# Lightning attention and a low-rank mixer on one core: new start of the pipeline and a new order of the attention steps

## The chip, the core and the metric

The kernel runs on one NeuronCore of a Trainium2 chip. The core has five engines that run side by side, each with an instruction queue of its own: TensorE (PE: matmuls, transposes as matmuls, and the weight loads that belong to them, shown apart as PEld), VectorE (DVE), ScalarE (ACT), GpSimd (POOL) and SyncE (SP), which here issues DMA transfers. ScalarE also issues some. An instruction waits in its queue until the semaphores it names have been raised, and what stands behind it on that engine waits with it.

The metric is the time of one execution on the device in microseconds (us). For the kernel before, three executions and one with the profiler are at hand. A trace of the profiled one gives the start and duration of each instruction, and for idle time of an engine a guess at what ended it.

## The reference

Two blocks follow each other. The first is a linear attention with a decay per head (4 batches, 8 heads, 768 positions, 64 channels), computed blockwise; the second mixes positions with a low-rank pair U, V and then applies a two-layer network.

```python
# attention, per block of positions (the kernel uses blocks of 128)
intra = einsum('bhic,bhjc->bhij', qb, kb) * Dmask        # Dmask[i, j] = lam ** (i - j), i >= j
intra = einsum('bhij,bhjd->bhid', intra, vb)
inter = einsum('bhid,bhde->bhie', qb * lam_pow, kv_state)
out   = intra + inter
kv_state = lam_block * kv_state + einsum('bhsd,bhse->bhde', kb * rev_pow, vb)
# bridge: x[b, s, h*64 + d]; then the mixer
u = x + (x.transpose(0, 2, 1) @ U @ V).transpose(0, 2, 1)
return u + maximum(u @ w_ch1, 0) @ w_ch2
```

q, k, v and lam are fp32. U (768x32), V (32x768), w_ch1 and w_ch2 are float64; the kernel loads them as pairs of 32-bit words and rebuilds fp32 values from exponent and mantissa bits.

## The kernel before

**Stages.** The attention front handles 24 steps s = 0..23 (4 batches of NT = 6 tiles of 128 positions); c = s % 6 is the place in the batch. After it come the first product (u @ w_ch1, in units of 12 or 24 matmuls of 128x512) and the second (with w_ch2). The trace puts the front at 0 to about 111 us, the first product's units from there. The change touches the front alone.

**What one step does.** The lists that the loop over s builds (`pieces`, printed below) are written out by hand, and each engine runs its instructions in that order. For step s, and always one step ahead for some of the work:

- `prep(s+1)`: PE transposes q and k of the next tile into one PSUM tile (`pqk`, L419); ScalarE copies them out as `qt`, `kt` (L425); SP issues the load of a later q.
- `scale(s+1)`: GpSimd makes `qs` = qt times powers (L450) and `ks` of the tile after (L439).
- `intra(s)` (L524): PE multiplies the masked scores `sm` with v into `px`. `inter(s)` (L536): PE adds qs times the state `kv` to `px`. `state(s)` (L489): PE makes k'v into `pkv`, VectorE forms the next state (L495, L497 or L500). In which order these three stand depends on s: `inter_first` lists the steps in which `inter` goes first, steps up to 6 put `state` ahead of `intra`, later ones `intra` ahead of `state`.
- `next_v`: ScalarE issues the next load of v. `take_x` (L546): ScalarE copies px out as x. `fade` (L459): ScalarE scales the state.
- `scores(s+1)` (L466): PE makes the scores `pss` of the next tile. `masked(s+1)` (L475): VectorE multiplies them with the mask, in two halves of 0.65 us, into `sm`.
- `low`, `low_rows`, `next_of_low` (L556, L589, L597, L598, L608): once per batch, the product with U, its rounding and its spreading. `mix`, `mixed` (L631, L643): the product with V, added to x. `turn`, `split`, `turned` (L694, L708, L709, L701): transposes of u for the first product.

**Conversions.** `weight_steps` turns float64 words into fp32 in steps: load(s) from SP (L149), `one` on VectorE (L170, L158) with two exponent operations on ScalarE (L177, L178), `two` (L188), `three` (L196, which waits for L178), `four` (L201). For V more follow: `five` (L787), the high part (ScalarE, L794), and the low part in two row groups, `low(1)` on VectorE and `low(3)` on GpSimd (both L798). A table gives each step a number, and `aside(s)` runs the steps of that number: before `masked(s+1)` in some steps, behind it in others. `late` is the place at which the ScalarE part runs; for U and V that is one step later or at the end of the same one.

**The start.** lam (8 numbers) is loaded into one partition, a matmul with a row of ones (L855) copies it to all 128, and VectorE moves it to `lamb` (L857). From that come the mask (eight scans, L367) and the powers (L379). Meanwhile PE runs matmuls of zeros, `keep_busy` (L402): two of 128x128, then after L855 two of 128x128 and nine of 16x16. The first loads are issued in the order q0 (two halves), q1, v0, k2, v1, q2, U, k3 on SP; lam, k0 (two halves), k1 on ScalarE's queue. Buffers: three for q, three for v, four for k.

Of the kernel before, what the change touches and what calls it, by code (L numbers as in the profile page):

```python
# [8 lines left out]
FP32 = mybir.dt.float32  # L9
# [5 lines left out]
P = 128  # L15
# [3 lines left out]
def kernel(  # L19
# [28 lines left out]
    nc = tc.nc  # L48

    B, H, S, D = q.shape  # L50
    HP = H // 2
    NT = S // P
# [7 lines left out]
    NS = B * NT  # L60
# [28 lines left out]
    def on_scalar(what):  # L89
        if late and late[0] is None:  # L90
            late.append(what)
        else:
            what()


    def set_ends(t):
        nc.vector.memset(t[:, 0:1], 1151.0)
        nc.vector.memset(t[:, 1:2], 255.0 * (1 << 23))
        ends.append(t)
# [202 lines left out]
    consts = att_ctx.enter_context(tc.tile_pool(name="consts", bufs=1))  # L302
# [7 lines left out]
    def two_banks(name, tag):  # L310
        return psf.tile([P, 2, N], FP32, tag=tag, name=name)
# [7 lines left out]
    def bank(shape, name, tag):  # L319
        return psa[0].tile(shape, FP32, tag=tag, bufs=2, name=name)  # L320

    lamb = consts.tile([P, H], FP32, name="lamb")
# [74 lines left out]
    def keep_busy(n):  # L397

        out = two_banks("idle", "pm")[:, 0]
        for i in range(n):  # L400
            k = P if i < 2 else D // 4
            nc.tensor.matmul(  # L402
                out=out[0:k, 0:k], lhsT=blank[:, 0:k], rhs=blank[:, 0:k], start=True, stop=True
            )
# [101 lines left out]
        del raw[s, "v"]  # L506
        load_next("v", nc.scalar)

    inter_first = (NT - 1, NT + 1, NS - 1)

    def px_of(s):
        if "px" not in st[s]:
# [38 lines left out]
    def low(b):  # L551

        pp = two_banks("pp", "px")[:, 0, 0:P] if b < B - 1 else bank([P, P], "pp", "b2")
        for c in range(NT):
            for g in range(G):
                nc.tensor.matmul(  # L556
                    out=pp[g * R : (g + 1) * R, :], lhsT=u_w[:, c, :],
                    rhs=xs[b * NT + c][:, g * P : (g + 1) * P],
                    start=(c == 0), stop=(c == NT - 1),
                )  # L560
        pps[b] = pp
# [152 lines left out]

    splits = {}

    pieces = [("prep", 0), ("next_k", 0), ("third_v", 0), ("scale", 0), ("scores", 0), ("masked", 0)]
    for s in range(NS):
        b, c = divmod(s, NT)
        done = s - NT - 1  # L720
        more = s + 1 < NS
        turns = done > 0 and (done - 1) // TG < FG
        mixes = 0 <= done < NS - NT - 1
        rows = c == 0 and b > 0
        step = [("fade", s)] * (c > 0)
        step += [("mix", done)] * (mixes and c != 1) + [("turn", done - 1)] * turns
        step += [("next_of_low", b - 1)] * rows
        step += [("split", done - 1)] * turns
        step += [("prep", s + 1)] * more
        step += [("mix", done + 1)] * (not more)  # L730
        step += [("scale", s + 1)] * more
        step += [("mixed", done)] * (mixes and c != 1)
        step += [("late", s - 1)] * (1 < s < NT - 1 or s > NT)
        step += [("turned", done - 2)] * (done > 1 and c == 1)
        step += [("mixed", done + 1)] * (not more)
        both = [("intra", s), ("state", s)] + [("v_low", s)] * (s == NT)
        if s in inter_first:
            step += [("inter", s)] + both + [("next_v", s)]
        else:
            step += (both if s > NT else both[1:] + both[:1]) + [("next_v", s), ("inter", s)]  # L740
        step += [("take_x", s)]
        step += [("next_of_low", b - 1)] * rows
        step += [("late", s)] * (s < 2 or s in (NT - 1, NT))
        step += [("turned", done - 1)] * (done > 0 and c > 0)
        step += [("mix", done), ("mixed", done)] * (mixes and c == 1)
        step += [("scores", s + 1)] * more
        step += [("low", b)] * (more and c == NT - 1)
        step += [("aside", s)] * (0 < s < NT - 2 or s > NT)
        step += [("masked", s + 1)] * more
        step += [("low_rows", b)] * (more and c == NT - 1)  # L750
        step += [("aside", s)] * (s in (0, NT - 2, NT - 1, NT))
        step += [("store", done)] * (done >= 0 and done // TG < FG)
        step += [("next_k", s)] * (s > 0)
        pieces += step
    waiting = {name: list(range(NS)) for name in "qkv"}

    def load_next(name, engine=nc.sync):
        if waiting[name]:
            load(name, waiting[name].pop(0), engine)


    run = {
        "prep": prep, "fade": fade, "scores": scores, "masked": masked, "inter": inter, "take_x": take_x,
        "intra": intra, "state": state,
        "low": low, "low_rows": low_rows, "next_of_low": next_of_low, "mix": mix, "turn": turn,
        "mixed": mixed, "store": store, "next_v": next_v, "split": lambda s: splits.pop(s)(),
        
        "next_k": lambda s: load_next("k"), "third_v": lambda s: load_next("v", nc.scalar), "scale": scale, "turned": lambda s: turned.pop(s)(),
    }
    def v_steps():  # L770

        st = {}

        def dst():
            if "v" not in st:
                st["v"] = wconv.tile([P, C], FP32, tag="wf", name="vf")[0 : 2 * R, 0:SH]
            return st["v"]

        def parts(gs):
            for half in range(2):  # L780
                rows, cols = slice(half * R, (half + 1) * R), slice(half * SH, (half + 1) * SH)
                for g in gs:
                    yield v_hl[g * R : (g + 1) * R, cols], rows

        def five():
            st["t"] = t = wconv.tile([P, C], FP32, tag="wt", name="vt")[0 : 2 * R, 0:SH]
            nc.vector.tensor_scalar(  # L787
                t.bitcast(U32), st["v"].bitcast(U32), HI, None, ALU.bitwise_and
            )
            on_scalar(high)  # L790

        def high():
            for out, rows in parts((0, 2)):
                nc.scalar.copy(out, st["t"][rows])  # L794

        def low(g, engine):
            for out, rows in parts((g,)):
                engine.tensor_tensor(  # L798
                    out=out, in0=st["v"][rows], in1=st["t"][rows], op=ALU.subtract
                )  # L800

        halves = [moe_V[:, half * SH : (half + 1) * SH] for half in range(2)]
        return weight_steps(dst, halves, SH, 2 * R, in_parts=True) + [
            five, lambda: v_low.append(lambda: low(1, nc.vector)), lambda: low(3, nc.gpsimd),
        ]

    v_low = []
    run["v_low"] = lambda s: v_low.pop()()


    u_side = weight_steps(
        lambda: u_w.rearrange("p c r -> p (c r)"), moe_U.rearrange("(c p) r -> p c r", p=P), NT * R
    )
    side = {}
    for steps, at in (
        (u_side, (-1, 1, 1, 2, 2)),
        (v_steps(), (0, 0, 3, 3, 4, 4, 4, 5, 5)),
        (w1_steps(0, True, True), (8, 9, 10, 11, 12, 14, 15, 16, 17, 17, 20, 21)),
        (w1_steps(1, True, True), (14, 15, 16, 17, 18, 22, 23, NS, NS, NS, NS, NS)),
    ):  # L820
        assert len(steps) == len(at)
        for step, n in zip(steps, at):
            side.setdefault(n, []).append(step)

    def aside(s):
        late.insert(0, None)
        for step in side.pop(s, ()):
            step()
        late.pop(0)
# [5 lines left out]

    ordered = ctx.enter_context(ExitStack())
    ordered.enter_context(tc.manual_schedule())
    lam_row = consts.tile([1, H + P], FP32, name="lam_row")
    blank = x_pool.tile([P, C], FP32, tag="x", name="blank")[:, 0:P]
    nc.vector.memset(blank, 0.0)  # L840
    nc.vector.memset(lam_row[:, H:], 1.0)
    set_ends(vp[:, S + C : S + C + 2].bitcast(FP32))
    nc.scalar.dma_start(out=lam_row[:, 0:H], in_=lam.unsqueeze(0))
    load_next("q", nc.sync)
    load_next("k", nc.scalar)
    load_next("q")
    load_next("k", nc.scalar)
    for name in "vkvq":
        load_next(name)
    aside(-1)  # L850
    load_next("k")
    make_identity(nc, ident)
    pl = two_banks("pl", "pss")[:, 0, 0:H]
    keep_busy(2)
    nc.tensor.matmul(out=pl, lhsT=lam_row[:, H:], rhs=lam_row[:, 0:H], start=True, stop=True)  # L855
    keep_busy(3 + 8)
    nc.vector.tensor_copy(out=lamb, in_=pl)  # L857
    constants()
    powers()
    nc.vector.tensor_copy(out=rev, in_=mask[:, :, :, P - 1])  # L860
# [646 lines left out]
```

## Time and profile before

| | |
|---|---|
| three executions | 635.54, 637.08, 637.39 us (median 637.08) |
| the profiled execution | 635.38 us, of which its span (first to last instruction) 633.6 us |
| VectorE busy | 467.1 us (74%) |
| ScalarE busy | 330.6 us (52%) |
| GpSimd busy | 147.7 us (23%) |
| DMA, mean over the span | 205 GB/s |
| DMA, 0 to 45 us | 230 GB/s, busy in nearly each slice from 2.5 to 29 us |

An engine's busy time is the union of its instructions' intervals; matmuls overlap in the pipeline and their ends are modelled. The list of waits names, for each idle stretch of an engine, the event that ended it; where an instruction waits for several, the last one is named, and it need not be the one that mattered. In the timeline each row is a run of like instructions: start, duration, engine, line, operation, output and inputs, count, and in brackets the idle time before it with its releaser. PEclk, the granted clock of TensorE, reads full in every slice.

### The profile page before, as it was taken

The page shows a single profiled execution, that of the slowest core. Times are in us where ns is not written, and L with a number is a line of the kernel's source. Part 1 is how long each engine was busy: PE and PEld are TensorE (multiplying, and loading weights), DVE is VectorE, ACT ScalarE, POOL GpSimd, SP SyncE. Part 2 cuts the span into 40 slices and gives each one's busy share as a digit, 9 for nine tenths or more (in the row PEclk, how much of TensorE's full clock was granted, in tenths as well). Part 3 has the DMA queues.
Part 4 walks back from the last instruction along what each step waited for, and adds up shares of the span by engine and source line. Part 5 has one row for each costly group of instructions (what it writes and reads, how often), then busy time and mean ns, then how long its engine had stood idle before and what let it go on. Part 6 is the DMA issues. An engine that isn't in the chain of part 4 may idle for free.

```text
span 633.6 us, 13669 instructions
## 1 busy us (share of the span) xinstructions
PE 625.8 (99%) x5213; PEld 528.1 (83%) x5213; DVE 467.1 (74%) x752; ACT 330.6 (52%) x604; POOL 147.7 (23%) x125
## 2 busy tenths in 40 slices
PE   8999999999999999999999999999999999999997
PEld 8989889888888888888888888888888888888886
DVE  6777888757888889797888799784665754855844
ACT  3775756636778777878777744322322322323220
POOL 4476887000000000000667500030210300300300
PEclk9999999999999999999999999999999999999999
DMA  9989995457898888755865796363353453532521
GB/s 229 256 216 257 256 241 143 138 186 267 314 336 281 308 293 283 278 190 182 275 227 197 260 315 204 118 233 100 116 208 94 143 188 100 194 131 92 182 84 66
DMA packets 141955, 129.61 MB, mean 205 GB/s; under 512 B 82562, under 2 KB 99970, under 8 KB 141890
## 3 DMA queue, kind: packets, MB, share of 16 engines
q1 hardware_dynamic: 116768, 122.32, 60.2%
q10 hardware_dynamic: 25122, 6.42, 4.5%
q8 instruction: 41, 0.67, 0.4%
q14 instruction: 24, 0.20, 0.1%
HBM read 79.04 MB, written 49.28 MB: 203 GB/s over the span
## 4 chain that ended last, share of the span: by engine, by line
PE 93%; DMA 3%; DVE 1%; SPq 1%; ACT 1%; issue 0%; POOL 0%; DVEq 0%; POOLq 0%
PE pz L986 24%; PE pz L1346 14%; PE pz L1348 14%; PE pd L1350 14%; PE z L986 5%; PE p L986 3%; PE px L524 3%; PE pss L466 3%; PE pz L914 2%; PE d L986 2%; PE c L986 2%; PE px L536 2%; DMA vraw<-in_v_dram 1%; PE pkv L489 1%; PE pqk L419 1%; PE pd L925 1%
## 5 line engine op out<-in xcount | busy, mean ns | idle before, releaser
L1322 ACT ACTIVATE m<-rm 128x512 fp32r<-128x512 f32 x96 | 60.6, 632 | 174.0 <-PE pd L1350 134.0
L1327 DVE SCALAR_TENSOR_TENSOR m<-rm,m 128x512 fp32r<-128x512 f32 x96 | 71.5, 746 | 80.9 <-ACT m L1322 80.9
L986 PE MATMUL pz<-u_hl,w 128*128 128x512 f32 x448 | 110.3, 389 | 0.0
L1346 PE MATMUL pz<-w_hl,m 128*128 128x512 f32 x264 | 102.7, 389 | 0.0
L1348 PE MATMUL pz<-w_hl,m 128*128 128x512 f32 x264 | 102.7, 389 | 0.0
L1350 PE MATMUL pd<-w_d,m 128*128 128x512 f32 (+1 forms) x267 | 101.4, 387 | 0.0
L986 PEld LDWEIGHTS pz<-u_hl,w 128*128 128x128 f32 x448 | 84.1, 188 | 17.5
L285 POOL TENSOR_TENSOR w<-w 128x512 fp32r<-128x512 f32 x29 | 40.5, 1414 | 210.8 <-DVE w L279 197.2
L1328 DVE SCALAR_TENSOR_TENSOR m<-m 128x512 fp32r<-128x512 f32 x96 | 74.8, 780 | 3.0
L1378 POOL TENSOR_TENSOR o<-o,u 128x512 f32<-128x512 f32 x20 | 29.8, 1517 | 198.5 <-DVE o L1374 198.5
L986 PE MATMUL pz<-u_d,w 128*128 128x512 f32 x224 | 59.9, 389 | 0.0
L1350 PEld LDWEIGHTS pd<-w_d,m 128*128 128x128 f32 x267 | 49.8, 188 | 10.3
L1348 PEld LDWEIGHTS pz<-w_hl,m 128*128 128x128 f32 x264 | 49.6, 188 | 10.3
L1346 PEld LDWEIGHTS pz<-w_hl,m 128*128 128x128 f32 x264 | 49.5, 188 | 10.2
L986 PEld LDWEIGHTS pz<-u_d,w 128*128 128x128 f32 x224 | 42.0, 188 | 8.7
L1346 PE MATMUL pz<-w,m 128*128 128x512 f32 x120 | 46.7, 389 | 0.0
L1348 PE MATMUL pz<-w,m 128*128 128x512 f32 x120 | 46.7, 389 | 0.0
L1350 PE MATMUL pd<-w,m 128*128 128x512 f32 x120 | 46.7, 389 | 0.0
L993 ACT ACTIVATE pz<-pz 128x512 f32<-128x512 f32 x56 | 32.5, 581 | 26.4 <-PE pz L986 26.4
L475 DVE TENSOR_TENSOR sm<-pss,mask 128x512 f32<-128x512 f32 x48 | 30.8, 684 | 16.2 <-PE pss L466 16.1
L997 ACT ACTIVATE r<-pz 128x512 f32<-128x512 f32 x56 | 33.3, 596 | 12.1 <-PE pz L986 11.5
L196 DVE SCALAR_TENSOR_TENSOR sc<-words,sc 128x512 uint32<-128x512 uint32 (+2 forms) x34 | 23.8, 700 | 17.3 <-ACT sc L178 17.3
(140 smaller groups left out, 1118.1 us busy)
## 6 DMA issues: line engine op xcount, KB each, us to landing
r_d<-r SPq DMA_DIRECT2D x96, 256.0 KB, 2.9
rm<-r_d SPq DMA_DIRECT2D x96, 256.0 KB, 2.6
words<-in_moe_w_ch_dram SPq DMA_DIRECT2D x30, 512.0 KB, 5.1
wf<-forms_d SPq DMA_DIRECT2D x56, 128.0 KB, 2.9
u_d<-x_nat SPq DMA_DIRECT2D x24, 256.0 KB, 3.6
u<-u_d SPq DMA_DIRECT2D x24, 256.0 KB, 4.5
qraw<-in_q_dram SPq DMA_DIRECT2D x23, 256.0 KB, 4.7
out_dram<-o SPq DMA_DIRECT2D x23, 256.0 KB, 2.0
```

The costliest lines, as they stand in the source:

```text
L285: engine.tensor_tensor(out=st["third"], in0=st["low"].bitcast(FP32), in1=st["hi"].bitcast(FP32), op=ALU.subtract,)
L475: nc.vector.tensor_tensor(out=sm[:, x], in0=pss[:, x], in1=mask[:, x], op=ALU.mult)
L986: nc.tensor.matmul(out=out, lhsT=weights, rhs=moving, start=start and i == 0, stop=i == len(pieces) - 1, skip_group_check=not start,)
L993: nc.scalar.mul(acc, acc, 1.0 + E)
L997: nc.scalar.mul(r, acc, 4096.0)
L1322: nc.scalar.activation(out=m[:, 0], in_=rs[i], func=AF.Relu, scale=NEAR)
L1327: nc.vector.scalar_tensor_tensor(m[:, 1], r, 0.0, hi, ALU.max, ALU.subtract)
L1328: nc.vector.scalar_tensor_tensor(m[:, 2], hi, E, low, ALU.mult, ALU.subtract)
L1346: nc.tensor.matmul(out=pz, lhsT=m[:, 0, cols], rhs=hi, start=first, stop=False)
L1348: nc.tensor.matmul(out=pz, lhsT=m[:, 1, cols], rhs=low, start=False, stop=end)
L1350: nc.tensor.matmul(out=pd[:, part], lhsT=m[:, 2, cols], rhs=third[:, part], start=first, stop=end, skip_group_check=part.stop != C,)
L1378: nc.gpsimd.tensor_tensor(out=o, in0=o, in1=u, op=ALU.add)
```

## The change

- lam goes to `lamb` in one DMA that writes all 128 partitions; the matmul L855, the copy L857 and one memset are gone.
- `keep_busy` runs once with 14 matmuls: six of 128x128 and eight of 16x16.
- The third q is loaded ahead of the second v; U's load moves behind the fourth k and q (it is now run by `aside(-1)` behind `prep(0)`).
- U's conversion steps move from 1, 1, 2, 2 to 2, 2, 3, 3; V's loads from step 0 to step 1, its `two` from 3 to 4, so that `aside(3)` holds U's `three` and `four` and V's `one`.
- Step 7 leaves `inter_first`: its order is now `intra`, `state`, `next_v`, `inter`.
- V's `low(1)` on VectorE moves from step 6's `state` to `aside(6)`, behind `masked(7)`.
- In steps 12 and 18 `aside` runs behind `masked`, not ahead of it. These hold `one` of two tiles of w_ch1.

```diff
-            k = P if i < 2 else D // 4
+            k = P if i < 6 else D // 4
...
-    inter_first = (NT - 1, NT + 1, NS - 1)
+    inter_first = (NT - 1, NS - 1)
...
-    pieces = [("prep", 0), ("next_k", 0), ("third_v", 0), ("scale", 0), ("scores", 0), ("masked", 0)]
+    pieces = [("prep", 0), ("aside", -1), ("next_k", 0), ("third_v", 0), ("scale", 0), ("scores", 0), ("masked", 0)]
...
-        both = [("intra", s), ("state", s)] + [("v_low", s)] * (s == NT)
+        both = [("intra", s), ("state", s)] 
...
-        step += [("aside", s)] * (0 < s < NT - 2 or s > NT)
+        aside_first = 0 < s < NT - 2 or s > NT and c > 0
+        step += [("aside", s)] * aside_first
         step += [("masked", s + 1)] * more
         step += [("low_rows", b)] * (more and c == NT - 1)
-        step += [("aside", s)] * (s in (0, NT - 2, NT - 1, NT))
+        step += [("aside", s)] * (not aside_first)
...
-            five, lambda: v_low.append(lambda: low(1, nc.vector)), lambda: low(3, nc.gpsimd),
+            five, lambda: low(3, nc.gpsimd), lambda: low(1, nc.vector),
...
-        (u_side, (-1, 1, 1, 2, 2)),
-        (v_steps(), (0, 0, 3, 3, 4, 4, 4, 5, 5)),
+        (u_side, (-1, 2, 2, 3, 3)),
+        (v_steps(), (1, 1, 3, 4, 4, 4, 4, 5, 6)),
...
-    lam_row = consts.tile([1, H + P], FP32, name="lam_row")
-    nc.vector.memset(lam_row[:, H:], 1.0)
-    nc.scalar.dma_start(out=lam_row[:, 0:H], in_=lam.unsqueeze(0))
+    nc.scalar.dma_start(out=lamb, in_=lam.unsqueeze(0).broadcast_to([P, H]))
...
-    for name in "vkvq":
+    for name in "vkqv":
         load_next(name)
-    aside(-1)
     load_next("k")
     make_identity(nc, ident)
-    pl = two_banks("pl", "pss")[:, 0, 0:H]
-    keep_busy(2)
-    nc.tensor.matmul(out=pl, lhsT=lam_row[:, H:], rhs=lam_row[:, 0:H], start=True, stop=True)
-    keep_busy(3 + 8)
-    nc.vector.tensor_copy(out=lamb, in_=pl)
+    keep_busy(14)
```

More of the change, by code (lines that the diff above doesn't have):

```diff
@@ L739 @@
         else:
-            step += (both if s > NT else both[1:] + both[:1]) + [("next_v", s), ("inter", s)]
+            step += (both if s > NT else both[::-1]) + [("next_v", s), ("inter", s)]
         step += [("take_x", s)]
@@ L803, in v_steps @@
         return weight_steps(dst, halves, SH, 2 * R, in_parts=True) + [
-            five, lambda: v_low.append(lambda: low(1, nc.vector)), lambda: low(3, nc.gpsimd),
+            five, lambda: low(3, nc.gpsimd), lambda: low(1, nc.vector),
         ]
-    v_low = []
-    run["v_low"] = lambda s: v_low.pop()()
     u_side = weight_steps(
```

## The prediction

> **What bounds the kernel now.** I read the page's first part, then the list of what TensorE waited for, then the chain of waits and the timeline at the places it names.
>
> ```profile
> PE 625.8 (99%) x5213; PEld 528.1 (83%) x5213; DVE 467.1 (74%) x752; ACT 330.6 (52%) x604; POOL 147.7 (23%) x125
> ...
> PE px L524 <- ACT qt L425: 1.5, 2, 0.8
> PE idle L402 <- DVE blank L840: 1.1, 1, 1.1
> PE px L536 <- POOL qs L450: 1.0, 1, 1.0
> PE pqk L419 <- DMA qraw<-in_q_dram: 0.4, 1, 0.4
> ```
>
> Columns of the waits: us in all, times, longest. TensorE is idle 633.6 - 625.8 = 7.8 us in the whole span; 2.9 of them (1.5 + 1.0 + 0.4) are stalls inside the front, the rest is the start, the end and crumbs. From 92 us on no wait of TensorE is listed, so what the front saves, the end should save: first-product units start right behind the front, and their weight part L239 ends at 121.84, over 9 us ahead of its first use at 131. That sets the size of the game: at most some 3 us of 637.
>
> The three places, from the timeline:
>
> ```profile
> 7.28 0.85 SPq L337 DMA_DIRECT2D qraw<-in_q_dram  x1
> 12.01 0.46 PE L419 MATMUL pqk<-ident,qraw 64*128 64x64 f32 x8 [0.43 <-DMA qraw<-in_q_dram]
> ...
> 36.04 1.46 POOL L450 TENSOR_TENSOR qs<-qt,powq 128x512 f32<-128x512 f32 x1
> 37.55 0.58 ACT L425 COPY kt<-pqk 128x512 f32<-128x512 f32 x1
> 37.56 0.69 PE L536 MATMUL px<-kv,qs 64*64 64x64 f32 x32 [0.95 <-POOL qs L450]
> 39.73 0.51 PE L631 MATMUL pm<-vp 64*128 64x256 f32 x4
> ...
> 62.99 1.04 DVE L170 TENSOR_SCALAR sc<-words 128x512 uint32<-128x512 uint32 x1
> 63.95 1.27 DVE L475 TENSOR_TENSOR sm<-pss,mask 128x512 f32<-128x512 f32 x2
> 64.59 0.59 ACT L425 COPY kt<-pqk 128x512 f32<-128x512 f32 x1
> 64.73 1.24 PE L524 MATMUL px<-vraw,sm 128*64 128x64 f32 x32 [0.71 <-ACT qt L425]
> ```
>
> At 12.01 the third q is late. At 37.56 `inter(7)` waits for qs, which stands on GpSimd behind L598. At 64.73 the list names qt, but the first half of sm ends at 63.95 + 0.64 = 64.6: the mask is what came late, and it came late because L170 stood in front of it. The same picture is at 90.29 to 92.04 in step 19.
>
> **Step 13 and step 19 (`aside` behind `masked`).** Scores of step 13 end at 63.27 and the state copy L495 at 63.07, so the mask can start at 63.3 and its first half ends at 63.95. TensorE is through with its transposes at 64.02 and starts `intra` there, 0.7 earlier. `intra` lasts 1.08 in the chain, to 65.1; `state` then needs the PSUM tile that kt is copied from, free at 64.59 + 0.59 = 65.18, so it starts at 65.25, against 65.80: 0.55 saved. What is late next: L170 runs behind the mask, from 64.6, and L709 behind it, about 65.2 as before; L643, which the next L631 needs, comes 0.5 earlier too. The exponents L177 wait for L170 and move from 65.07 to 65.25; ScalarE's next work, x, is due at 66.5, where L178 ends 0.2 later. I take 0.5 for each step, 0.25 to 0.6 as bounds: 1.0 together.
>
> **Step 7 (`intra` first, V's low part behind the mask).** L798 on VectorE took 1.28 us (35.09 to 36.37) ahead of the mask, whose scores end at 36.11. Without it the mask starts at 36.15, its first half ends at 36.8, and `intra(7)` starts at 36.85 in place of `inter` at 37.56. It ends at 37.95; `state` waits for kt to 38.13 and runs 38.2 to 38.67 (0.47 in the chain); `inter` 0.62, to 39.3; L631 follows at 39.3 against 39.73 to 39.80. L631 needs V's low part: 1.28 behind the mask, 37.45 to 38.73, in time by 0.5; and the spread rows of L608, whose last issue at 36.3 landed 2.2 to 2.6 later, at 38.9, in time by 0.4. qs (37.5) is then no longer waited for. I take 0.45; bounds 0.1 (L608 or L798 late) to 0.55.
>
> **The start.** The third q takes v1's place in SP's queue, issued at 5.38 rather than 7.28; loads there took 4.6 to 5.6 us to land, so 10.0 to 11.0: the 0.43 us wait goes. v1 takes q2's place and lands at about 7.28 + 4.6 = 11.9; `state(1)` wants it at 12.65 - gain. That caps the gain of the start at about 0.7.
>
> The blanks cost more. A 128x128 blank is two records; four records took 1.15 us (2.73 to 3.88), so six blanks take 12 x 0.288 = 3.45, and eight small ones 16 x 0.033 = 0.53. From 1.05 that ends at 5.0, against 4.47 now. The first k half lands just before 4.96 and the second before 5.76, and both stop TensorE today (0.20 and 0.29), so much of that is covered: four groups of transposes at 0.27 from 5.0 end 0.3 later. If all goes on at today's rates, 0.3 of the 0.43 is given back: gain 0.1. The other end lies in these rows, weight loads of the scores of step 0 and of step 1:
>
> ```profile
> L466 PEld LDWEIGHTS pss<-qt,kt x16: 282/330/330, 6.2 to 7.6; 64*128 64x128 f32 x16
> ...
> L466 PEld LDWEIGHTS pss<-qt,kt x16: 183/188/188, 10.4 to 11.2; 64*128 64x128 f32 x16
> ```
>
> Until about 8.6 us TensorE runs at some 0.57 of its later rate, though the granted clock reads 1.00. If denser blanks end that earlier, the scores of step 0 (2.08 us) shrink towards 1.16; then k1 (landing 7.8), ks (GpSimd from 7.56) and v0 (2.40 + 5.8 = 8.2) come last, and the start gains the capped 0.7. [...] The rows before show the change of rate but not what triggers it. I take the middle of 0.1 and 0.7: 0.4.
>
> lam by 128 rows has no row. Nearest: the one-row load, issued at 0.73, was read at 2.21 (1.5 us), and the first q half of 128 partitions landed in 2.4, so lamb is there at 2.2 to 3.2; the scans start at 3.11 now. ks, their first reader, starts at 7.56 and ends at 8.6, with 0.25 us to its matmul at 8.87; the first mask waits 0.83 us for scores anyway. So -0.1 to +0.1, and delay of the k halves queued behind it at most 0.2: taken as 0. SP's k2 waits for lam's semaphore but reaches it at 3.04.
>
> **U and V.** No instruction is added; they change place. `aside(2)`: L170, L158, L188 ran 0.72 + 1.15 + 0.36, the first two beside GpSimd's instructions and ending with them; from 17.86 that gives about 20.2, and the mask started at 20.25. `aside(3)` puts L196, L201 and V's L170, L158 ahead of the mask of step 4 (24.29 now). L196 waits for U's L178, now behind kt(4) on ScalarE; but ScalarE is rid of L177, L178 a step earlier, so x(2) moves from 20.17 to 18.95, qt(4) from 21.62 to 20.6, kt(4) ends at 21.7 and L178 at 22.65. Then 0.36 + 0.36 + 0.34 + 0.34 alone on VectorE: 24.1. Cover: 0.2 us to 24.29 and 0.15 more before TensorE feels it. L158 took 1.42 where it met GpSimd's qs; that would cost up to 0.8 here. `aside(4)` adds L188's 0.55 behind the mask of step 5, and VectorE's 2 us idle there take it: 29.35 + 0.55 + 0.56 + 0.55 + 0.35 = 31.36, when the next scores end (31.30); L798 on GpSimd starts 0.5 later and L598 about 0.05 later. Loads: V goes behind q5 as well. SP issued 1,216 KB from 8.18 to V at 14.91, 181 KB per us; 1,472 KB now stand ahead, so V is issued at 16.3 and 17.4 and lands (4.9 to 5.2) at 22.3, wanted at 23.0. U lands at about 16, wanted at 17.9. Taken 0; bounds 0 to 0.8 lost.
>
> **Sum.** 1.0 + 0.45 + 0.4 + 0 + 0 = 1.85 us. Bounds by the terms: 2 x 0.25 + 0.1 + 0.1 - 0.8 = -0.1 (a small loss) to 1.2 + 0.55 + 0.7 = 2.45. The profiled execution took 635.38 (span 633.6 and 1.78 around it), so 633.5 on its terms. It is 1.7 below the median, 637.08; the four executions known average 636.35, and on that I put the forecast: 634.5.
>
> **Rivals.**
> Early clock: the start gives 0.7 and the sum 2.15, time 634.2. For it: twelve dense records in a row, and the rate does change within 9 us. Against: today's blanks and transposes fill 1.05 to 8.6 nearly too. Chance 0.2.
> Eaten gains: blanks end late, lam's rows push the k halves back 0.2 (start 0), steps 13 and 19 give 0.25 each because kt and L643 are next, step 7 0.45: 0.95 saved, 635.4. For it: each of these is within 0.5 us. Chance 0.2.
> The other side, V's words: L170 of V now stands ahead of the mask of step 4 and waits for two loads behind 256 KB more. The mask must start by 24.05 (24.45 less the start's 0.4), so with 0.7 for L170 and L158 the words must be there by 23.35; each us later goes straight into TensorE's time. At 25.2 the gains are used up; at 27.5 it is 2.3 slower, 638.7. For it: DMA is full up to 29 us and landings reached 6.5 us. Against: I reckon 22.3. Chance 0.1.
>
> **How the numbers follow.** The forecast has 0.5. About 0.3%, 1.9 us, is what a measurement here can tell from no change, and the forecast sits on it, 1.85 from the average and 2.6 from the median: faster by more 6 times in 10, in the early-clock case 8, in the eaten case 1. Faster: 0.5 x 0.6 + 0.2 x 0.8 + 0.2 x 0.1 = 0.48; slower 0.1; within 0.42. Executions spread from 635.38 to 637.39, so the range goes from the lowest less 2.45 (632.9) to the highest less 0.2 (637.2); it leaves out the other side and some of the tails.
>
> **What would show it.** Right: the four waits of TensorE listed above are gone or under 0.2; L631 first at 39.3 less the start's gain; the mask ahead of L170 at steps 13 and 19, `state` there 0.5 earlier relative to the scores; first-product units from about 109.3. The blanks ending at 5.0 and score weight loads of step 0 at 330 ns would show the plain start, 188 ns the early clock. Wrong: a new wait of TensorE at px in step 4, a VectorE wait for DMA of V's words, L631 waiting for L608, or a first-product unit waiting for its weights.

## The result, and the profile after

| | before | after |
|---|---|---|
| median of six executions each | 636.88 us (635.54 to 638.25) | 646.74 us (643.58 to 650.89) |
| the profiled execution | 635.38 us, span 633.6 | 643.58 us, span 641.8 |
| first-product units start | 111.21 | 119.41 |

The changed kernel is slower: ratio 1.0151, 95% interval 1.013 to 1.0173. The forecast of 634.5 and its range, up to 637.2, are missed, and on the other side of the time before. The units start 8.20 us later, and the span is 8.2 us longer: all of it is lost in the front and handed on to the end unchanged.

The busy line of the page after, its line for the loads of q (issues, KB each, median us from issue to landing; it read 4.7 before), and the list of what TensorE waited for (us in all, times, longest):

```profile
PE 627.6 (98%) x5213; PEld 528.5 (82%) x5213; DVE 468.2 (73%) x750; ACT 331.0 (52%) x604; POOL 147.2 (23%) x125
...
qraw<-in_q_dram SPq DMA_DIRECT2D x23, 256.0 KB, 6.2
```

```profile
PE pqk L419 <- DMA qraw<-in_q_dram: 2.9, 5, 0.9
PE pkv L489 <- DMA vraw<-in_v_dram: 1.3, 2, 0.8
PE idle L402 <- DVE blank L837: 1.1, 1, 1.1
PE pss L466 <- DVE kv L497: 0.9, 1, 0.9
PE pqk L419 <- DMA kraw<-in_k_dram: 0.8, 3, 0.4
PE pm L631 <- DMA vp<-vp: 0.8, 3, 0.4
PE px L524 <- ACT qt L425: 0.7, 1, 0.7
```

The busy times have hardly moved; what is new are waits of TensorE for loads. Before, one load in the whole span stopped it, for 0.43 us; now ten loads of q, k and v do, for 5.0 us. The table by stage says why. Columns: window, its length, TensorE busy (instructions), granted clock, DMA share, GB/s. The DMA share adds up the times of all packets over the 16 engines, so it can pass 1. Before:

```profile
2.00:4.00 2.00, 2.00 (x12) 1.00 0.94 212
6.00:8.00 2.00, 2.00 (x20) 1.00 1.27 287
8.00:20.00 12.00, 11.57 (x314) 1.00 1.15 263
20.00:38.00 18.00, 17.02 (x492) 1.00 1.00 227
```

After:

```profile
2.00:4.00 2.00, 2.00 (x13) 1.00 0.53 115
6.00:8.00 2.00, 1.40 (x22) 1.00 1.34 220
8.00:20.00 12.00, 8.70 (x223) 1.00 1.33 220
20.00:38.00 18.00, 16.58 (x480) 1.00 1.19 216
```

Two things stand there. From 6 us on DMA is busier than before (1.33 against 1.15) and yet moves less: a flat 220 GB/s, where it reached 287. And between 2 and 4 us it moves half of what it did. The timeline of the start, after:

```profile
4.22 2.63 DVE L367 TENSOR_TENSOR_SCAN mask<-lamb,ident 128x128 f32<-128x128 f32 x8 [3.21 <-DMA lamb<-in_lam_dram]
...
10.16 0.69 PE L489 MATMUL pkv<-vraw,ks 128*64 128x64 f32 x16 [0.83 <-DMA vraw<-in_v_dram]
...
13.75 0.46 PE L419 MATMUL pqk<-ident,qraw 64*128 64x64 f32 x8 [0.88 <-DMA qraw<-in_q_dram]
14.02 0.44 PE L419 MATMUL pqk<-ident,kraw 64*128 64x64 f32 x8
14.89 0.69 PE L489 MATMUL pkv<-vraw,ks 128*64 128x64 f32 x16 [0.43 <-DMA vraw<-in_v_dram]
```

The scans start at 4.22 (3.11 before), `state(0)` at 10.16 (8.87), the transposes of the third tile at 13.75 (12.01) in spite of the third q's earlier place. The scores of step 2 start 2.2 us later than before, those of step 5 4.6, of step 12 5.7, of step 23 8.0: the loss grows fastest while DMA is full.

What the diff does not say: **`lam_row` was a tile of 544 bytes per partition, the last of its pool, and the pool of q, k and v lies right behind.** With it gone, those tiles and all of the front behind them (ks, qt, kt, sm, x, the words of U, V and w_ch1) move down by 544 bytes. The addresses in the two built programs:

```
first tile of     before     mod 256    after      mod 256
q                 121600     0          121056     224
k                 127744     0          127200     224
v                 135936     0          135392     224
words             167680     0          167136     224
```

Each load of q, k or v writes rows of 64 fp32 values, 256 bytes, eight to a partition. Theory: a row that does not start at a multiple of 256 bytes in the destination costs the DMA more. As an estimate from the two rates, spread over 16 engines, 287 GB/s are 16 x 256 / 287 = 14.3 ns a row, 220 GB/s are 18.6 ns.

### The profile page after: what moved, and what is told of

Read it like the earlier page. It is cut to its first block, busy times and chain, and to the rows that moved or that the text cites. A ratio compares the mean times of both kernels' runs of the same rounds, so it can differ in the third digit from the quotient of the medians.

```text
span 641.8 us, 13665 instructions
## 1 busy us (share of the span) xinstructions
PE 627.6 (98%) x5213; PEld 528.5 (82%) x5213; DVE 468.2 (73%) x750; ACT 331.0 (52%) x604; POOL 147.2 (23%) x125
## 4 chain that ended last, share of the span: by engine, by line
PE 90%; DMA 3%; DVE 3%; ACT 1%; issue 1%; POOL 0%; SPq 0%; ACTq 0%; DVEq 0%; POOLq 0%
PE pz L977 24%; PE pz L1339 14%; PE pz L1337 14%; PE pd L1341 13%; PE z L977 5%; PE p L977 3%; PE pss L466 2%; PE pz L905 2%; PE d L977 2%; PE px L524 2%; PE c L977 2%; DMA vraw<-in_v_dram 1%; PE pd L916 1%; PE pqk L419 1%; DMA qraw<-in_q_dram 1%; PE px L536 1%
## 5 line engine op out<-in xcount | busy, mean ns | idle before, releaser
L196 DVE SCALAR_TENSOR_TENSOR sc<-words,sc 128x512 uint32<-128x512 uint32 (+2 forms) x34 | 23.1, 678 | 17.9 <-ACT sc L178 17.9
```

## The experiments

Each ratio is to runs of the kernel before beside it on the same chip. A step is counted from the start of its scores to the start of the next ones. Unused tiles set the addresses.

| kernel | q, k, v mod 256 | lam | ratio (95%) | GB/s in 6 to 8 us |
|---|---|---|---|---|
| after | 224 | 128 rows | 1.0151 (1.013 to 1.0173) | 220 |
| e1 after + 544 B | 0 | 128 rows | 1.0016 (0.9995 to 1.0036) | 287 |
| e2 before + 32 B | 32 | matmul | 1.0125 (1.0102 to 1.0148) | 220 |
| e3 before, lam by 128 rows | 0 | 128 rows | 1.0015 (0.9999 to 1.003) | 288 |
| e4 after + 96 B | 64 | 128 rows | 1.0166 (1.0133 to 1.0199) | 220 |
| e5 after + 160 B | 128 | 128 rows | 1.0107 (1.0074 to 1.0139) | 223 |
| e6 after, lam as before | 0 | matmul | 1.0008 (0.9991 to 1.0025) | 287 |
| e7 before, steps 12 and 18 | 0 | matmul | 0.998 (0.9965 to 0.9996) | 285 |
| e8 before, step 7 | 0 | matmul | 0.9994 (0.9975 to 1.0012) | 285 |
| e9 before, q, k, v alone + 32 B | 32 | matmul | 1.0115 (1.0096 to 1.0134) | 221 |
| e10 before, all behind them + 32 B | 0 | matmul | 1.0003 (0.9991 to 1.0015) | 288 |
| e11 e7 + third q ahead | 0 | matmul | 0.9999 (0.9989 to 1.0009) | 289 |
| e12 e11 + U's and V's steps | 0 | matmul | 0.9995 (0.9983 to 1.0006) | 286 |

**Is it the place of the tiles?** First the changed kernel with the 544 bytes given back, and the kernel before with 32 bytes too many:

```diff
     powq = consts.tile([P, HP, P], FP32, name="powq")
+    consts.tile([P, 136], FP32, name="spare")            # e1, on the kernel after
```

> The changed kernel with an unused tile of 544 bytes per partition in the place of the row of lam that the change took away, so that the tiles of q, k, v and of U's and V's words start at the addresses of the kernel before (multiples of 256) and not 544 lower (32 above a multiple of 64). No instruction differs. Theory 'placement' (the loads are slow because their target tiles start at an odd multiple of 32): DMA moves 280 to 290 GB/s from 8 to 20 us as before, not 218, and the time is 634 to 637, ratio 0.995 to 1.0. Rival 'broadcast' (the load of lam into 128 partitions slows the queues) and rival 'order' (late words, moved loads): 645 to 649, ratio about 1.015, DMA at 218 GB/s.

```diff
     lam_row = consts.tile([1, H + P], FP32, name="lam_row")
+    consts.tile([P, 8], FP32, name="spare")              # e2, on the kernel before
```

> The kernel before with an unused tile of 32 bytes per partition, which puts the tiles of q, k, v and the words 32 above a multiple of 64; nothing else differs. Placement: DMA falls from 287 to about 218 GB/s between 8 and 20 us, TensorE gets waits for q and v, and the time rises by 6 to 12 us (ratio 1.01 to 1.02). Broadcast and order: no change, ratio 1.000 within 0.002.

e1 takes 639.13 us beside 638.67 for the kernel before, e2 646.47. One unused tile makes the kernel before as slow as the change, and one takes nearly all of the change's loss away. The table by stage of e2:

```profile
6.00:8.00 2.00, 2.00 (x20) 1.00 1.39 220
8.00:20.00 12.00, 9.05 (x200) 1.00 1.34 218
```

and of e1:

```profile
2.00:4.00 2.00, 2.00 (x13) 1.00 0.53 115
6.00:8.00 2.00, 1.98 (x20) 1.00 1.27 287
8.00:20.00 12.00, 11.33 (x302) 1.00 1.14 258
```

e2 has the rate of the changed kernel. In e1 the 287 GB/s are back; the 115 GB/s between 2 and 4 us stay, so that is another matter (lam, below).

**How coarse is the grain?** Two more offsets, the changed kernel with 24 and with 40 fp32 values of unused tile:

```diff
+    consts.tile([P, 24], FP32, name="spare")             # e4: 64 above a multiple of 256
+    consts.tile([P, 40], FP32, name="spare")             # e5: 128 above it
```

> The changed kernel with an unused tile of 96 bytes, which puts the same tiles 64 above a multiple of 256: a multiple of 64, not of 128 or 256. Placement with a grain of 64 bytes: as the one padded with 544 bytes, 634 to 637 and 280 to 290 GB/s. Placement with a grain of 128 or 256 bytes: slow, 642 to 650. Broadcast and order: 645 to 649.

> The changed kernel with an unused tile of 160 bytes, so that q, k and v land 128 bytes above a multiple of 256. If the grain of the writes is 256 bytes (theory): DMA at 218 to 220 GB/s in 6 to 20 us as at offsets of 32, 64 and 224, ratio 1.012 to 1.017. If it is 128 bytes: DMA at 258 GB/s and more there, ratio 0.999 to 1.004, as with 544 bytes.

Both stay slow (648.49 and 646.51 us), at 219 and 220 GB/s in 8 to 20 us; e5's 1.0107 lies a little below what was expected, its interval reaches into it. With e2 and the changed kernel that makes four offsets, 32, 64, 128 and 224, with one rate: 218 to 220. Of the offsets tried only a multiple of 256 is fast (258 GB/s in e1, 263 before), and how far a row is from it makes no difference that these rates show.

A row of 256 bytes that does not start at a multiple of 256 lies across one wherever it starts, and the runs show one price for that: by the estimate above 18.6 ns in place of 14.3, with 32 of its bytes behind the boundary (e2) as with 224 (the changed kernel). What in the DMA makes such a row dearer, no run shows.

**Which tiles?** In e9 only the tiles of q, k and v are off, in e10 everything behind them and not they:

```diff
+    raw_pool.tile([P, 8], FP32, tag="spare", bufs=1, name="spare")   # e9
+    att.tile([P, 56], FP32, tag="spare", name="spare_att")           # e9
...
+    att.tile([P, 8], FP32, tag="spare", name="spare")                # e10
```

> The kernel before with an unused tile of 32 bytes ahead of the tiles that q, k and v are loaded into, and one of 224 bytes behind them: only the load targets leave the multiples of 256, all other tiles stay at one. Theory (the loss comes from the writes of q, k and v alone): DMA at 218 to 220 GB/s in 6 to 20 us, ratio 1.010 to 1.014. Rival (the tiles that the engines work on, or the words of U, V and w_ch1, have a share): ratio 1.004 to 1.009.

> The mirror: the targets of q, k and v stay at multiples of 256, and the tiles behind them (ks, qt, kt, sm, qs, the state, x, the words of U, V and w_ch1) are moved up by 32 bytes. Theory: DMA at 257 GB/s and more in 8 to 20 us, ratio 0.999 to 1.002. Rival: ratio 1.003 to 1.008.

e9, 644.64 us beside 637.47:

```profile
6.00:8.00 2.00, 2.00 (x22) 1.00 1.38 221
8.00:20.00 12.00, 9.57 (x222) 1.00 1.36 228
```

e10, 637.35:

```profile
6.00:8.00 2.00, 2.00 (x22) 1.00 1.28 288
8.00:20.00 12.00, 11.40 (x304) 1.00 1.18 266
```

The loads of q, k and v carry it all. Engines that work on tiles 32 bytes off, and loads of U, V and w_ch1 into such tiles, cost nothing that shows (e10, 1.0003). The 228 of e9 in its second window lies above the 218 to 220 that the expectation named; the time is within it.

**lam by 128 rows.** The kernel before with that edit alone, and the changed kernel without it:

```diff
-    lam_row = consts.tile([1, H + P], FP32, name="lam_row")
+    consts.tile([P, H + P], FP32, name="spare")          # e3: keeps the addresses
...
-    nc.scalar.dma_start(out=lam_row[:, 0:H], in_=lam.unsqueeze(0))
+    nc.scalar.dma_start(out=lamb, in_=lam.unsqueeze(0).broadcast_to([P, H]))
...
-    nc.tensor.matmul(out=pl, lhsT=lam_row[:, H:], rhs=lam_row[:, 0:H], start=True, stop=True)
-    nc.vector.tensor_copy(out=lamb, in_=pl)
```

> The kernel before with lam loaded into 128 partitions by one DMA, without the matmul and the copy, and with an unused tile that keeps all other addresses. Placement: little change, lamb comes later (read at some 3.5 to 4.2 rather than copied at 3.0), at most 1 us, ratio 0.999 to 1.002; DMA at 280 to 290 GB/s from 8 us on. Broadcast: most of the loss, ratio 1.01 to 1.017, and 218 GB/s.

```diff
-    nc.scalar.dma_start(out=lamb, in_=lam.unsqueeze(0).broadcast_to([P, H]))
+    nc.scalar.dma_start(out=lam_row[:, 0:H], in_=lam.unsqueeze(0))   # e6, with its tile, matmul and copy
...
-    keep_busy(14)
+    keep_busy(2)
+    nc.tensor.matmul(out=pl, lhsT=lam_row[:, H:], rhs=lam_row[:, 0:H], start=True, stop=True)
+    keep_busy(4 + 8, 4)                                   # four of 128x128, eight of 16x16
+    nc.vector.tensor_copy(out=lamb, in_=pl)
```

> The changed kernel with lam loaded into one partition and spread by the matmul and the copy again; the row tile is back, so the load targets are multiples of 256 again; all else as changed (14 blanks, q ahead of v, U and V, the steps). Theory (placement is most of the loss, the broadcast of lam another 1 us, the other edits gain about 1 together): ratio 0.996 to 0.999, first-product units from 110 to 111. Rival (one of the other edits loses about what steps 13 and 19 gain, as the late units of the kernel with 544 bytes, 114.1, may say): ratio 1.000 to 1.003, units from 111.2 or later.

The timeline of e3:

```profile
4.18 2.63 DVE L367 TENSOR_TENSOR_SCAN mask<-lamb,ident 128x128 f32<-128x128 f32 x8 [3.16 <-DMA lamb<-in_lam_dram]
...
8.62 2.08 POOL L439 TENSOR_TENSOR ks<-kraw,small 128x512 f32<-128x512 f32 x2 [7.32 <-DVE small L856]
...
9.74 0.48 PE L489 MATMUL pkv<-vraw,ks 128*64 128x64 f32 x8 [0.41 <-POOL ks L439]
```

lam, issued at 0.73, is there 3.4 us later, where one row took 1.5; the chain scans, powers, ks moves by 1.07, and `state(0)` goes from 8.87 to 9.74. Between 2 and 4 us five profiles with this edit (after, e1, e3, e4, e5) show 113 to 117 GB/s, nine with one row (before, e2, e6 to e12) 184 to 214. In the whole time e3 measures 1.0015 (0.9999 to 1.003): some 1 us, at the edge of what can be told from nothing. e6 was to be faster than before in the theory and is not: 639.16 against 638.79, where the rival had put it. So either one of the other edits costs something, or their gains do not come.

**The steps by themselves.**

```diff
-        step += [("aside", s)] * (0 < s < NT - 2 or s > NT)
+        aside_first = 0 < s < NT - 2 or s > NT and c > 0             # e7, on the kernel before
+        step += [("aside", s)] * aside_first
...
-        step += [("aside", s)] * (s in (0, NT - 2, NT - 1, NT))
+        step += [("aside", s)] * (not aside_first)
```

> The kernel before with one edit: in steps 12 and 18 the conversion stands behind the mask. By the prediction's term: the mask of steps 13 and 19 starts right behind the scores, 0.5 us saved in each, units from 110.2, ratio 0.9984. Rival (ScalarE's copies of q and k, or the conversions' own readers, are next): 0.5 or less together, units from 110.7 or later, ratio 0.999 to 1.000.

```diff
-    inter_first = (NT - 1, NT + 1, NS - 1)
+    inter_first = (NT - 1, NS - 1)                                   # e8, on the kernel before
...
-            five, lambda: v_low.append(lambda: low(1, nc.vector)), lambda: low(3, nc.gpsimd),
+            five, lambda: low(3, nc.gpsimd), lambda: low(1, nc.vector),
...
-        (v_steps(), (0, 0, 3, 3, 4, 4, 4, 5, 5)),
+        (v_steps(), (0, 0, 3, 3, 4, 4, 4, 5, 6)),
```

> The kernel before with one edit: step 7 multiplies the masked scores first and V's low part on VectorE stands behind the mask. By the prediction's term: 0.45 us saved at step 7, units from 110.8, ratio 0.9993. Rival (VectorE's low part there runs beside GpSimd's qs and ks and takes 2.7 us in place of 1.28, as in the changed kernel, so that the state and the mixed tile behind it come late): a loss of 0.2 to 0.8 us at the next product with V, ratio 1.0003 to 1.0012.

Lengths of some steps in us, by the starts of the scores ("no edit": none in steps 12 and 18):

```
step            12      13      18      19      7
before          5.26    5.22    5.26    5.28    5.12
after           5.82    4.80    5.55    5.50    5.28
e1              5.65    4.88    5.47    4.76    4.83
e3 (no edit)    5.76    4.76    6.06    4.76    5.12
e6              5.59    4.96    5.26    4.76    6.42
e7              6.08    4.75    5.26    4.76    5.09
e8 (no edit)    5.26    5.24    5.27    5.21    5.89
e9 (no edit)    6.64    4.76    6.09    4.75    5.10
e10 (no edit)   5.27    5.22    5.26    5.27    5.09
e11             5.26    4.75    5.83    4.88    5.12
```

Where the step before it ran undisturbed (5.26), step 19 of e7 is 4.76 in place of 5.28 and step 13 of e11 4.75 in place of 5.22: 0.5 each, as predicted, and e7's ratio of 0.998 says 1.3 us, though the medians (638.69 beside 638.79) differ by 0.1 only. But e3 and e9, which have not this edit, show 4.75 and 4.76 too, behind steps that TensorE took 0.5 to 1.4 longer over: while TensorE stands, VectorE gets through L170, and the edit has nothing left to save.

Step 7 is another picture. The timeline of e6 (e8 shows the same, with a wait of 0.79 in the row of L631):

```profile
37.03 1.24 PE L524 MATMUL px<-vraw,sm 128*64 128x64 f32 x32 [0.35 <-issue]
37.56 2.71 DVE L799 TENSOR_TENSOR vp<-vf,vt 32x384 fp32r<-32x384 f32 x2
...
38.29 0.69 PE L489 MATMUL pkv<-vraw,ks 128*64 128x64 f32 x16
...
38.90 0.69 PE L536 MATMUL px<-kv,qs 64*64 64x64 f32 x32
...
39.53 0.38 PE L631 MATMUL pm<-vp 64*128 64x256 f32 x1
...
41.23 0.50 PE L631 MATMUL pm<-vp 64*128 64x256 f32 x3 [1.32 <-DMA vp<-vp]
```

The new order does run earlier: `intra` 2.00 us behind the start of the scores, `state` 3.26, L631 4.50 (4.78 before). But the first L631 runs and the other three wait for rows that L608 spreads. Of its four issues on SP one took 1.44 us here and 1.78 in e8, where 0.78 was the longest before, and the slowest landed 4.0 and 4.1 us after its issue where it was 2.6. The step takes 5.89 and 6.42 us instead of 5.12. In e1, e4 and e5 no L608 is late, and it takes 4.83, 4.86 and 4.81. TensorE waits for these rows in three of the six profiles with the edit (the changed kernel, e6, e8) and in none of the eight without it. That the edit itself makes the landing late is not shown: e7, without it, has an issue as long (1.77 us) whose rows were there within 2.5. Nor does the time of e8, 0.9994 (0.9975 to 1.0012), show a change. V's low part (L799 here, L798 before) took 1.28 us before, 2.4 to 3.0 in e6, e8 and the changed kernel, beside GpSimd's ks and qs; it makes the state's copy L497 late, which nothing in TensorE's list shows here. Before, most of its time lay beside GpSimd's L598 (33.51 to 35.96), and it took 1.28 all the same; what lengthens it beside ks and qs, no run shows.

**A version that beats both?** The edits that had held, on the kernel before, without and with the new steps of U and V:

```diff
-    for name in "vkvq":
+    for name in "vkqv":                                              # e11, with the edit of e7
...
-        (u_side, (-1, 1, 1, 2, 2)),
-        (v_steps(), (0, 0, 3, 3, 4, 4, 4, 5, 5)),
+        (u_side, (-1, 2, 2, 3, 3)),                                  # e12, with U's load behind prep(0)
+        (v_steps(), (1, 1, 3, 4, 4, 4, 4, 5, 5)),
```

> The kernel before with two edits: conversion behind the mask in steps 12 and 18, and the third q ahead of the second v. Expected: about 0.5 us saved in each of steps 13 and 19 (4.76 us from scores to scores in place of 5.22 and 5.28) and 0.4 to 0.6 in step 1 (3.8 in place of 4.40): 1.4 to 1.6 us, ratio 0.9975. Rival (v then is as late as q was): step 1 at 4.2 or more, ratio 0.998 to 0.999.

> The same with the new steps of U and V (V's low part on VectorE stays where it was, and so does step 7). If they cost nothing, as predicted: steps 2 to 6 add up to the same or to 0.2 us less each where a stall of 0.2 stands now, ratio 0.997 to 0.9975. Rival (V's words ahead of the mask of step 4): a wait of TensorE at px in step 4 and 0.3 to 0.8 us more than the kernel without them, ratio 0.998 to 0.999.

Neither differs measurably from the kernel before (637.05 and 637.28 us beside 637.47), so the expected 0.25% did not come. e12's profile, with TensorE at its full rate from about 8.3 us (8.6 before), has the scores of step 2 at 14.11 (14.82 before): 0.28 of the 0.71 was there at the scores of step 0 already, and the other 0.43 is the wait for the third q. In e11 TensorE ran slowly until about 10.7 (weight loads of 227 ns from 10.0 to 10.5 us, 138 from 11.0) and step 2 starts at 15.02. Whether e7's 0.998 is a gain stays open, since e11 holds the same edit and shows none.

## Why the prediction was wrong

**The step that failed** is the one on lam: the sum weighed the DMA, the matmul and the copy ("taken as 0") and did not ask what else the removed tile did. Its 544 bytes kept the loads of q, k and v on multiples of 256. That is worth 1.0125 (e2) or 1.0115 (e9) by itself, 7 to 8 us, four times all the gains of the sum. The mechanism was neither in the sum, the bounds nor the rivals, so no chance stood for the side on which the result fell, but for the 0.1 of V's words.

**lam's own time was mis-sized.** Forecast at 2.2 to 3.2 us, it came at 4.1. The bound of 0.1 on `state(0)` was 0.87 (e3), because ks was not ready with time to spare: 1.07 later at its start was more than the 0.25 us to its matmul. SP's issue of the third k, which by the prediction's own note waits behind lam, also moved, from 3.04 to 4.10 in e3.

**Steps 13 and 19 held.** In the changed kernel the mask starts 0.05 us behind the end of the scores (68.36 + 1.16) and L170 behind it (step 13):

```profile
69.57 1.29 DVE L475 TENSOR_TENSOR sm<-pss,mask 128x512 f32<-128x512 f32 x2 [0.67 <-PE pss L466]
70.36 1.24 PE L524 MATMUL px<-vraw,sm 128*64 128x64 f32 x32
70.77 0.42 DVE L170 TENSOR_SCALAR sc<-words 128x512 uint32<-128x512 uint32 x1
```

L170 takes 0.42 there, 1.04 before. The size, 0.5 a step, was right for a run in which nothing else stops TensorE; the rows of e3 and e9 show that such a run was assumed.

**Step 7 failed on its cover.** The forecast left L608's rows 0.4 us to spare, on landings of 2.2 to 2.6. The issues took up to 1.0 us longer than in the one trace it came from, and the gain of 0.45 is one of 0.3 in the step (e1, e4, e5) or a loss of 0.8 to 1.3 (e8, e6). "L631 waiting for L608" had been named as the sign. Whether the edit or the run makes the rows late stays open.

**The start.** The third q's wait of 0.43 is saved where the loads are fast (e12), but under slow loads q is late wherever it stands. The blanks end at 4.52, not at 5.0: twelve records of a run without a break took 0.245 us each (3.47 less 16 x 0.033, by 12), and not the 0.288 taken from a shorter one. The forecast's working for the plain start also slips: its groups of 0.27 from 5.0 end the fourth at 6.08, and today's fourth, started at 5.76, ends at 6.03, so kt(0) would be 0.05 later and not 0.3. Of the two rates, weight loads of the scores of step 0, after:

```profile
L466 PEld LDWEIGHTS pss<-qt,kt 64*128 64x128 f32 x16 | 1.1, 188 | 0.4 <-ACT kt L425 0.4
```

and e1, with the same fourteen blanks:

```profile
L467 PEld LDWEIGHTS pss<-qt,kt 64*128 64x128 f32 x16 | 1.9, 320 | 0.0
```

Columns: busy us, mean ns of one, idle time before. The same blanks gave the early rate (188 ns) once and the late one (320) once, so neither case is settled by them: the time at which the rate changes differs from run to run. That denser blanks bring the change forward, which the 0.7 in the start's term supposes, no run shows: they ended at 4.52 in both, and only one of the two had the full rate then. The changed kernel had the full rate as the blanks ended: its four transposes at 4.79 took 0.34 us, e1's at 4.71 took 0.48. And e1's transposes at 8.71 still took 0.64, where 0.42 is the full rate. The early rate gained nothing in the changed kernel, because `state(0)` then waited 0.83 us for v.

**U and V held in part.** e6 went as forecast: L178 ends 0.28 us ahead of the scores of step 4, and the mask follows them at once. Steps 2 to 4 take 3.79, 3.94 and 3.79 us there, against 4.01, 4.00 and 4.02 before. In the other five profiles with the new steps (after, e1, e4, e5, e12) L178 ends about 0.8 us behind the start of these scores. The changed kernel:

```profile
26.70 1.16 PE L466 MATMUL pss<-qt,kt 64*128 64x128 f32 x16
27.03 0.46 ACT L178 ACTIVATE sc<-sc,vp 128x192 uint32<-128x192 f32 x1
27.52 0.36 DVE L196 SCALAR_TENSOR_TENSOR sc<-words,sc 128x192 uint32<-128x192 uint32 x1 [1.38 <-ACT sc L178]
...
28.85 1.27 DVE L475 TENSOR_TENSOR sm<-pss,mask 128x512 f32<-128x512 f32 x2
...
29.67 1.19 PE L524 MATMUL px<-vraw,sm 128*64 128x64 f32 x32 [0.69 <-ACT qt L425]
```

VectorE's L196 waits 1.38 us for L178, the mask starts 0.99 behind the end of the scores, and TensorE waits 0.69 at px. The row names qt, but px starts 0.82 us behind the mask's start, just as before (24.29 and 25.11), so it is the mask. This is the sign that the prediction had named, and the loss lies within its bound of 0.8; it came through ScalarE and not through V's words. x(2) was to move to 18.95; it starts at 19.27 in e6, but at 20.04 in e12 and 20.98 in e1. In e1, e4, e5 and e12 a stop of TensorE inside these scores, of 0.7 to 1.9 us, covers the late mask (the stops are the next point).

**The base.** In the profile of before no stall of TensorE in the front is put down to "issue", a stop for which the profile shows no cause. In all thirteen others there are 0.6 to 6.2 us of them, at places that change (not counted: the 0.35 at px in step 7, with the edit there, which is the mask). In e1:

```profile
23.54 0.93 PE L467 MATMUL pss<-qt,kt 64*128 64x128 f32 x11
25.86 0.60 PE L467 MATMUL pss<-qt,kt 64*128 64x128 f32 x5 [1.39 <-issue]
```

A group of sixteen matmuls stops in its middle for 1.39 us. The sum was made on a trace that had none, so its half microseconds were sized for a run that is rarer than the median. That trace is of the fastest kind too: 635.38 us, where the kernel before took 637.47 to 638.79 beside the experiments, and it was not profiled there.

The traces tell more of these stops. Count TensorE's records (weight loads, matmuls, semaphore instructions) in order of start: every one of the 61 stops of the thirteen profiles stands ahead of a record whose number, divided by 256, leaves 193 (195 in two). So they come only at one place in each 256 records. The page lists a DMA queue of the kind "instruction" with 41 packets, 16,384 bytes each by the trace, and 41 x 256 is 10,496, as many records as TensorE has in e1 (10,545) but for 49. Each stop ends 1.2 to 1.75 us after the landing of such a packet, and at none of the some 300 such places, with a stop or without, does TensorE go on sooner than 1.19 us after it. In e1 the packet of 22.55 us took 1.99 (most take 0.9 to 1.3), and the stop ended at 25.86. The reading that fits these counts is that TensorE waits there for its own instructions, which that queue brings; the page does not say whose they are, no run changed it, and what makes a packet late is not shown. The stops add up to 3.9 to 6.2 us in four of the kernels with slow loads (e2, e4, e5, e9), to 0.6 to 2.9 in the eight with fast ones, and to 0.6 in the changed kernel: a part of what slow loads cost can lie in these stops, and in e2 it is more than the waits for loads (3.4 us).

## What to carry to other kernels

Removing, adding or resizing a tile moves every tile that is allocated behind it: before costing such an edit, compare the start addresses of the DMA targets, and where rows of 256 bytes are loaded keep them on multiples of 256, with an unused tile if need be (287 GB/s here, 220 off them). A DMA share that rises while GB/s fall is the sign (here, in 8 to 20 us, from 1.15 to 1.33, and from 263 to 220 GB/s); where DMA bounds the start, look at it before any wait. And half a microsecond taken from the waits of a single trace should be held against a second one, since stops elsewhere can have the same microsecond already. At a stop called "issue" in the middle of a group, count TensorE's records up to it: all 61 here kept to one place in each 256, which speaks for a late packet of instructions and not for the data.

## What the runs showed of the hardware that was not expected

- Rows of 256 bytes into SBUF at 32, 64, 128 and 224 above a multiple of 256 move at 218 to 228 GB/s with DMA full (6 to 20 us), on a multiple at up to 289; the offset's size makes no difference.
- A load of 32 bytes into each of 128 partitions landed 3.4 us after its issue (one row: 1.5), and meanwhile DMA moved half as much (115 against 212 GB/s) at about half the share (0.53 against 0.94).
- TensorE's change from its slow to its full rate after the start came between 4.8 us at the latest (the changed kernel) and about 10.7 (e11), at a granted clock of 1.00 (4 to 6 us of the changed kernel) and 0.999 (mean over e11's span).
- In two of the kernels with slow loads the granted clock fell: 0.86 in 8 to 20 us of e4, 0.81 in 20 to 38 us of e5. Both are kernels in which TensorE waited for loads; the others of that kind read 1.00 (the changed kernel in 8 to 38 us, e2 and e9 over the span).
- TensorE stopped 61 times in thirteen profiles, up to 1.94 us (e5), at one place in each 256 of its records. The DMA queue of the kind "instruction" moved 41 packets of 16,384 bytes, about one for 256 of these records, and none of the stops ended less than 1.2 us after such a packet had landed. That TensorE waited there for its instructions is the reading of these counts.
